# Attention and a long convolution in one kernel: zero columns by the planned share, kv cleared in pieces, kv stored in load order, part A in pairs

## The chip, the core and the metric

The kernel runs on one core of one Trainium2 chip. The metric is the device time of one execution in microseconds (us). The kernel before takes 856.5 us, the median of 7 runs (855.29 to 857.41).

## What is computed

Two independent parts write the two halves of the output's last axis. S is 2048, D is 640, and all data are bf16.

```
part A:  k_shift[t] = sum over j<4 of k[t-j] * shift_k[:, j]
         kv         = k_shift * v
         y          = causal convolution of kv with ssm_k, channel by channel, over 2048 steps (by FFT)
         a          = q * (y + kv * ssm_D)
part B:  q, k, v    = x @ wqkv, 32 heads of 20 channels
         p          = softmax(q k^T / sqrt(20)), 2048 x 2048 for each head
         b          = (p v) @ wo
output   = concat(a, b) on the last axis, (1, 2048, 1280)
```

## The kernel before, in words

**An order written by a planner.** The kernel is one straight program for each engine. While it is built, the class `Prog` keeps a modelled clock for each engine (`P.T`), and every operation is added with a modelled cost `c`. A loop (L1240) looks at the modelled clock of TensorE and decides what comes next on it. Once written, the order on every engine is fixed: if an operation is slower on the chip than its `c`, everything queued behind it on that engine is late. Nothing is rearranged at run time.

**Part B.** There are 512 blocks (4 query chunks of 512, 8 groups of 4 heads, 16 key blocks of 128), each with 4 units, one for each head: 2048 units in all. For a unit, TensorE computes scores of 128 keys by 512 queries into one PSUM bank (S_task, L619), and an exponential is taken of them. ScalarE does this for 2 or 3 banks in one instruction (EXP_task, L661). Some units are given to VectorE instead, which takes the exponential in six or seven steps: the first reads PSUM (L681), the others work in SBUF on two units at a time (`chain_end`, L711 to L721). The results lie in 36 slots of SBUF until PV_task (L739) multiplies them with v and frees the slots. `want_vec` (L1150) says when VectorE gets a unit: only if its modelled lead and backlog are below VQ us, and only in the earlier key blocks of a group (KBW, and KBV for a pair that is already open).

**Work beside it.** The projections for q, k and v (L473, L522), the short filter of part A ("C" tasks, L550, with a multiplication by v on VectorE, L570), the output projection (L825) and the long convolution (L974) have due times in blocks and are put between the scores. The C tasks are due at block KV0 + KVS * n for n = 0 to 19. C tasks multiply by diagonal matrices Dg, which GpSimd builds with one instruction (L592) from the identity and the filter's weights SK.

**The long convolution.** After the last projections of k and v, the space of the weights is used again (`conv_setup`, L915). 40 tasks of 128 matmuls each (5120 matmuls, L974) multiply Toeplitz pieces of ssm_k, loaded by DMA (`hk_load`, L938), with kv. kv goes through HBM: VectorE's products are stored as rows in `kvr_scratch` (L564), loaded back 80 channels at a time (`kvr_load`, L933) and regrouped on GpSimd (`kvx_build`, L943). In each matmul the moving operand has n = 16 - d positions for two halves; it is doubled by a second set of columns that are zeros (KVZ). The doubled columns add zeros to the neighbouring results: they change no value. Only the first matmul of a task has no such columns. Part of the tile for kv must be zero and is cleared by one GpSimd instruction (L926).

**Columns that keep TensorE streaming.** The planner counts how long TensorE streams columns in the last 3.4 us (`share`, L1221). Where there is slack and the count is below ZTH, it adds matmuls on a tile of zeros (`zeros`, L381); ahead of a convolution step it adds one if the count is below ZLO.

**Order on GpSimd and VectorE.** GpSimd operations of the convolution wait in a list and are put beside a VectorE operation that reads PSUM (`pool_beside`, L428). A VectorE step marked "two" (those in SBUF) is planned not to start while GpSimd is planned busy.

**Part A's end.** For each 160 channels, 16 tiles of q (128 rows by 160) are loaded, multiplied by y on GpSimd (L1015), and stored (`A_start`, L1003). Six tiles are allocated and four are in flight.

**SyncE** issues nearly all DMAs in the order written; each waits for its own semaphore's DMA before it. x is loaded transposed: four tiles of 128 rows, then three of 512 rows (L400 to L405).

Of the kernel before, what the change touches and what calls it, by code (L numbers as in the profile page):

```python
# [25 lines left out]
NAQ = 6  # L26
# [4 lines left out]
OBS = 20  # L31
NXB = 3
KBV, KBW, LONE = 13, 12, 16
CQ = 0.026
KV0, KVS, VQ, CONVE, ZTH, AGE, WAIT3 = 52, 2.5, 5, 80, 2.1, 40, 0.2
ZST = 6
# [4 lines left out]
PKX, PAT = 0.56, 0.42  # L41
DMAX = 2.0
ZSL, ZLO = 0.45, 1.8
# [43 lines left out]
class Prog:  # L87
# [140 lines left out]
    def dmas(self, eng, pairs, dsem, reads=(), writes=(), slow=1, turn=False):  # L228
# [18 lines left out]
        c = 0.475 * len(pairs)  # L247
# [29 lines left out]
def build_kernel(nc, A_q, A_k, A_v, A_shift_k, A_ssm_k, A_ssm_D, B_x, B_wqkv, B_wo, out):  # L277
# [3 lines left out]
    with ExitStack() as es:  # L281
# [30 lines left out]
        HK_E, KVR_E, KVX_E, Y_E, AST_E = 4 * HKW, 64 * 80, 16 * 64, 16 * 160, 160  # L312
# [37 lines left out]
        kvr_d = nc.dram_tensor("kvr_scratch", (S, D), BF16).ap()  # L350
# [49 lines left out]
        for t in range(4):  # L400
            x_load(t, 1)
        x_load(4, 4)
        w_load("sp", [(WKV, D, 2, 0, 160), (WKV, 0, 1, 80, 80), (WQ, 0, 0, 80, 80)], b_Wa, "wa")
# [81 lines left out]
        def prologue():  # L485

            def two(bw, bd):

                bd.w = [t for b in bw for t in b.w]
                bd.r = []  # L490
            for _ in range(ZST):
                zeros(0, 1, True)
            KQ_mm("K", 0, MISC, 0, 384)
            hq, hk = [Buf(), Buf()], [Buf(), Buf()]
            for i, (bk, eng) in enumerate(((4, "dve"), (3, "act"))):
                KQ_mm("Q", 0, bk, 256 * i, 256)
                if i == 0:
                    copy("act", KT[:, 0, 0:384], bank[MISC][:, 0:384], bkb[MISC], hk[0], 0.6)
                copy(eng, QT[:, 0, 256 * i:256 * (i + 1)], bank[bk][:, 0:256], bkb[bk], hq[i], 0.45)
            KQ_mm("K", 0, 5, 384, 128)  # L500
            copy("dve", KT[:, 0, 384:512], bank[5][:, 0:128], bkb[5], hk[1], 0.35)
            two(hq, b_QT[0])
            two(hk, b_KT[(0, 0)])
# [29 lines left out]
        d_kvr, d_sk, d_kext, d_small = DS("kvr"), DS("sk"), DS("kext"), DS("small")  # L533
# [6 lines left out]
        def C_task(c, h, bk):  # L540
# [18 lines left out]
            def after():  # L559
                if h < 4:  # L560
                    return
                for t in range(4):
                    bd = Buf()
                    P.dma("sp", ap(kvr_d, [[32 * D, 4], [-D, 32], [1, D]], (c * 512 + t * 128 + 31) * D), kvst[i][:, t, :],  # L564
                          d_kvst[i], reads=[b_kvst[i]], writes=[bd])
                    b_kvd.append(bd)
# [5 lines left out]
        def setup_pool():  # L572
# [3 lines left out]
            P.dma("sp", SK, ap(A_shift_k, [[KS, 128], [128 * KS, NCC], [1, KS]]), d_sk, writes=[b_SK])  # L576
            k_load(0)
            k_load(1)
# [13 lines left out]
            P.op("pool", lambda e: e.tensor_tensor(  # L592
                Dg, ap(ident, [list(ident.ap[0]), [0, KS], [0, NCC], [1, 128]]),
                ap(SK, [list(SK.ap[0]), [1, KS], [KS, NCC], [0, 128]]), ALU.mult), reads=[b_ident, b_SK], writes=[b_Dg], c=6.0)
# [320 lines left out]
        def conv_setup():  # L915
# [10 lines left out]
            P.op("pool", lambda e: e.memset(KVr[:, 0:48, :], 0.0), writes=[cv["KVr"]], c=48 * 80 * 0.00095)  # L926
# [6 lines left out]
        def kvr_load(b):  # L933
            P.dmas("sp", [(KVr[32 * a:32 * a + 32, 16 * a:64, :],
                           ap(kvr_d, [[D, 32], [32 * D, 64 - 16 * a], [1, 80]], 80 * b)) for a in range(4)],
                   d_kvr, reads=b_kvd, writes=[cv["KVr"]], slow=2)
# [6 lines left out]
        def kvx_build(t):  # L943
            i = t % 2
            for h in range(2):
                dst = sub(KVX[i].bitcast(U32), [[64, 4], [16, 4], [1, 16]], 256 * h)
                src = sub(KVr2, [[1, 4], [40, 4], [160, 16]], t % 5 * 8 + 4 * h)
                pool_work(lambda e, dst=dst, src=src: e.tensor_copy(dst, src), [cv["KVr"]], [cv["KVX"][i][h]], PKX,  # L948
                          lambda h=h: kvr_load(t // 5 + 1) if h and t % 5 == 4 and t < 39 else None)
# [5 lines left out]
        def conv_task(bt):  # L955
# [3 lines left out]
            for u in range(4):  # L959
# [3 lines left out]
                for x in range(4):  # L963
                    for k in range(8):
# [6 lines left out]
                        rhs = sub(KVX[i], [[(2 - i) * KVX_E - p, 1 if st else 2], [64, 2], [2, n]], p)  # L971
                        o = sub(bank[MISC], [[-16 if u + x else 16, 1 if st else 2], [256, 2], [1, n]], (4 * u + x) * 16 + d)
                        yield (CQ, rd if x + k == 0 else [])
                        P.op("pe", lambda e, o=o, lhsT=lhsT, rhs=rhs, st=st, k=k: e.matmul(  # L974
                            o, lhsT, rhs, start=st, stop=k == 7, skip_group_check=True),
                            reads=rd, writes=[bkb[MISC]], tok=last, c=CQ, st=4 * n / 2400)
# [22 lines left out]
        def A_load(B, tp):  # L999
            i = tp % NAQ  # L1000
            P.dma("sp", Aq[i], ap(q2, [[D, 128], [1, 160]], tp * 128 * D + 160 * B), d_aq[i], writes=[cv["Aq"][i]])

        def A_start(B):  # L1003

            def go(tp):
                i = tp % NAQ
                q = cv["Aq"][i]
                A_load(B, tp)

                def after():  # L1010
                    P.dma("sp", ap(out2, [[2 * D, 128], [1, 160]], tp * 128 * 2 * D + 160 * B), Aq[i], d_ao[i], reads=[q])
                    if tp + NAQ - 2 < 16:
                        go(tp + NAQ - 2)

                pool_work(lambda e, a=Aq[i], y=Y[B % 2][:, tp, :]: e.tensor_tensor(a, a, y, ALU.mult), [q, cv["Y"][B % 2]], [q], PAT,  # L1015
                          after)

            for tp in range(NAQ - 2):
                go(tp)
# [99 lines left out]
        def dve_run(until):  # L1119
            while True:  # L1120
# [8 lines left out]
                if True:  # L1129
                    fn, rd, wr, c, two = w.steps[w.i]  # L1130
                    t = last_dve[0]
# [289 lines left out]
```

## Time and profile before

| what | value |
|---|---|
| median of 7 runs | 856.5 us |
| the profiled execution | 855.89 us |
| its span on the core | 853.2 us (2.7 us lie around it) |
| first exponential starts | 10.19 us |
| last exponential ends | 843.8 us |
| mean granted TensorE clock | 0.994 |
| exponentials on ScalarE | 465 of 2 units, 276 of 3, 1 of 1 (1759 units) |
| exponentials on VectorE | 289 units |
| convolution on TensorE | from 238.1 to 802.2 us |
| matmuls on zeros (L381) | 230 |
| HBM traffic | 106.83 MB read, 10.61 MB written |

"Span" is from the first to the last instruction. A row of a group of instructions gives: line, engine, operation, the tiles written and read, the shape, the count, then busy time in us and mean ns of one, then the idle time of the engine just before them and what ended it. In rows of the timeline, the numbers are start in us, length in us; square brackets hold the engine's idle time before it. Names such as R stand for the big working space, PS for PSUM, XV and XF for VectorE's own tiles. A busy share of TensorE says little here, since each matmul's record lasts some 390 ns for 512 columns while the next one starts about 215 ns later.

### The profile page before, as it was taken

What the parts mean: (1) busy time and instruction counts of PE and PEld (TensorE: products, weight loads), DVE (VectorE), ACT (ScalarE), POOL (GpSimd) and SP (SyncE); (2) the same over time, 40 slices, a digit from 0 to 9 for tenths busy, and PEclk for the clock granted to TensorE, in tenths of its full rate; (3) what the DMA queues carried; (4) which work ended last, traced back from release to release, by engine and by line L of the source; (5) the groups of instructions that cost most, each with busy time, mean ns of one, the idle gap of its engine ahead of it and who ended that gap; (6) DMA issues with size and microseconds to landing.
All of it is one profiled execution on the core that took longest, in us unless ns stands there. A gap on an engine that the chain in (4) does not pass through costs nothing.

```text
span 853.2 us, 27281 instructions
## 1 busy us (share of the span) xinstructions
PE 819.1 (96%) x11683; PEld 380.6 (45%) x11694; DVE 775.2 (91%) x1560; ACT 811.1 (95%) x748; POOL 96.6 (11%) x160
## 2 busy tenths in 40 slices
PE   8979999999999999999999999999999999999997
PEld 3433433442255454444534544554544554455422
DVE  2388999999989999998999999999999999999992
ACT  5878799999999999999999999999999999999996
POOL 2020000000111000012211010220110121100011
PEclk9989999999999999999999999999999999999999
DMA  9920211211749977978888796789798888988411
GB/s 182 292 61 2 42 54 22 73 33 32 145 111 204 179 171 171 186 167 186 193 163 175 166 209 140 175 199 195 176 188 158 199 191 194 164 185 181 77 31 46
DMA packets 189463, 121.91 MB, mean 143 GB/s; under 512 B 98048, under 2 KB 188672, under 8 KB 189344
## 3 DMA queue, kind: packets, MB, share of 16 engines
q1 hardware_dynamic: 187152, 117.06, 64.5%
q0 software_dynamic: 736, 2.75, 0.9%
q8 instruction: 92, 1.51, 0.8%
q10 hardware_dynamic: 1456, 0.37, 0.2%
q14 instruction: 27, 0.22, 0.1%
HBM read 106.83 MB, written 10.61 MB: 138 GB/s over the span
## 4 chain that ended last, share of the span: by engine, by line
PE 50%; ACT 33%; DVE 15%; issue 1%; DMA 0%; SPq 0%; DVEq 0%
ACT R L661 33%; PE PS L974 17%; PE PS L619 15%; PE PS L739 7%; PE PS L473 5%; DVE XV L681 4%; DVE XF L721 2%; PE PS L825 2%; PE PS L381 1%; PE PS L522 1%; DVE XF L716 1%; DVE R L711 1%; DVE ZS L991 1%; DVE ZS L990 1%; DVE R L993 1%
## 5 line engine op out<-in xcount | busy, mean ns | idle before, releaser
L661 ACT ACTIVATE R<-PS 128x1024 bf16<-128x1024 f32 (+1 forms) x742 | 807.6, 1232 | 26.8 <-PE PS L619 25.2
L619 PE MATMUL PS<-QT,KT 20*128 20x512 bf16 x2048 | 288.3, 386 | 19.2 <-ACT R L661 6.9
L974 PE MATMUL PS<-R 128*128 128x60 bf16 (+4 forms) x5120 | 212.1, 195 | 0.2 <-DVE R L993 0.2
L681 DVE TENSOR_SCALAR XV<-PS 128x512 uint16<-128x512 f32 x289 | 197.2, 684 | 16.0 <-PE PS L619 13.3
L974 PEld LDWEIGHTS PS<-R 128*128 128x128 bf16 x5120 | 176.0, 98 | 79.0 <-issue 77.7
L739 PE MATMUL PS<-R,V_sb 128*21 128x512 bf16 x2048 | 168.2, 385 | 5.3 <-DVE R L711 2.5
L619 PEld LDWEIGHTS PS<-QT,KT 20*128 20x128 bf16 x2048 | 71.9, 91 | 192.8 <-ACT R L661 132.9
L721 DVE TENSOR_TENSOR XF<-XF 128x1024 bf16<-128x1024 bf16 x145 | 98.7, 682 | 0.3
L718 DVE TENSOR_TENSOR XF<-XF 128x1024 bf16<-128x1024 bf16 x145 | 98.2, 681 | 0.2
L948 POOL COPY R<-R 128x256 uint32<-128x256 uint32 x80 | 51.1, 639 | 377.5 <-DVE XF L721 114.1
L739 PEld LDWEIGHTS PS<-R,V_sb 128*21 128x21 bf16 x2048 | 37.8, 89 | 78.3 <-issue 40.6
L381 PE MATMUL PS<-Zt 128*128 128x512 bf16 x230 | 68.5, 393 | 1.6 <-DVE Zt L375 1.0
L716 DVE TENSOR_SCALAR XF<-XV 128x1024 uint16<-128x1024 uint16 x145 | 64.5, 452 | 0.2
L711 DVE TENSOR_TENSOR R<-XF,XV 128x1024 uint16<-128x1024 bf16 x92 | 62.8, 685 | 0.2
L719 DVE TENSOR_SCALAR XF<-XF 128x1024 bf16<-128x1024 uint16 x145 | 60.2, 417 | 0.4
L717 DVE TENSOR_SCALAR XF<-XF 128x1024 bf16<-128x1024 uint16 x145 | 59.7, 418 | 0.1
L473 PE MATMUL PS<-xT,WQ 128*20 128x512 bf16 (+1 forms) x660 | 50.0, 380 | 0.9 <-DVE XV L681 0.7
L473 PE MATMUL PS<-xT,R 128*20 128x512 bf16 (+2 forms) x660 | 47.8, 382 | 1.8 <-DMA xT<-in_B_x_dram 1.3
L1015 POOL TENSOR_TENSOR R<-R 128x160 bf16<-128x160 bf16 x64 | 31.2, 488 | 160.6 <-DVE XF L719 50.8
L713 DVE TENSOR_TENSOR R<-XF,XV 128x512 uint16<-128x512 bf16 x105 | 40.4, 418 | 0.1
L462 DVE CAST KT<-PS 128x512 bf16<-128x512 f32 (+1 forms) x32 | 21.6, 675 | 13.8 <-PE PS L473 13.4
L749 DVE CAST OT_sb<-PS 128x512 bf16<-128x512 f32 x32 | 21.8, 681 | 12.8 <-PE PS L739 12.8
(54 smaller groups left out, 359.8 us busy)
## 6 DMA issues: line engine op xcount, KB each, us to landing
R<-kext_scratch SPq DMA_DIRECT2D x640, 136.0 KB, 3.7
R<-in_A_v_dram SPq DMA_DIRECT2D x4, 640.0 KB, 6.2
kext_scratch<-in_A_ssm_k_dram POOLq DMA_DIRECT2D x1, 2560.0 KB, 13.3
kvr_scratch<-R SPq DMA_DIRECT2D x16, 160.0 KB
R<-kvr_scratch SPq DMA_DIRECT2D x8, 320.0 KB, 6.1
R<-in_A_q_dram SPq DMA_DIRECT2D x64, 40.0 KB, 3.4
out_dram<-R SPq DMA_DIRECT2D x64, 40.0 KB, 2.8
R<-kvr_scratch SPq DMA_DIRECT2D x8, 240.0 KB, 7.0
```

What stands on the lines that cost most here:

```text
L381: P.op("pe", lambda e: e.matmul(bank[bk], Zt, zrhs, start=start, stop=start, skip_group_check=True), reads=[b_Zt], writes=[bkb[bk]], tok=s ...
L473: ins = e.matmul(bank[bk][32 * i:32 * i + DH, 0:n], Wt[:, cc, off + i * DH:off + (i + 1) * DH], xT[:, cc, x0:x0 + n], start=(cc == 0), sto ...
L619: ins = e.matmul(bank[b0 + i], KT[32 * u:32 * u + DH, g, kb * 128:(kb + 1) * 128], QT[32 * u:32 * u + DH, qs(qc, g), :], start=True, stop= ...
L661: P.op("act", lambda e: e.activation(P_sb[:, s0:s0 + m, :], PS[:, b0 * 512:(b0 + m) * 512].rearrange("p (u q) -> p u q", u=m), ACT.Exp, sc ...
L681: work(0.2, [(lambda e: e.tensor_scalar(V, bank[bk], scale * 1.4426950408889634 * 128.0, 127.0 * 128.0, op0=ALU.mult, op1=ALU.add), [bkb[b ...
L711: last = [(lambda e: e.tensor_tensor(o, Q2, V2, ALU.add), bv + [bq], [b_P[z] for z in zs], two, True)]
L716: (lambda e: e.tensor_scalar(F.bitcast(U16), V, 127, None, op0=ALU.bitwise_and), bv, [bf], one, True),
L718: (lambda e: e.tensor_tensor(Q, Q, F.bitcast(U16), ALU.mult), [bf, bq], [bq], two, True),
L719: (lambda e: e.tensor_scalar(F, F.bitcast(U16), a / 16384.0, b / 128.0, op0=ALU.mult, op1=ALU.add), [bf], [bf], one, True),
L721: (lambda e: e.tensor_tensor(Q, Q, F, ALU.mult), [bf, bq], [bq], two, True)] + last, end)
L739: ins = e.matmul(bank[OBANK][32 * u:32 * u + DH + 1, :], V_sb[:, kb, 4 * g + u, :], P_sb[:, slot[4 * b + u], :], start=first, stop=last, t ...
L974: P.op("pe", lambda e, o=o, lhsT=lhsT, rhs=rhs, st=st, k=k: e.matmul(o, lhsT, rhs, start=st, stop=k == 7, skip_group_check=True), reads=rd ...
```

## The change

The computation is the same. These parts change.

1. **Convolution matmuls** are doubled with zero columns only for d = 1 and 2, and only if `share` is below ZDU = 2.1 at that point. They are costed at CQ = 0.0258 (not doubled) or CQD = 0.0304 (doubled), where all had 0.026.
2. **Planner constants.** The filling of zeros: ZTH 2.1 to 2.2, ZLO 1.8 to 1.4, ZSL 0.45 to 0.3. C tasks: KV0 52 to 56, KVS 2.5 to 3.0. Convolution paced to end 100 units before the end, not 80. VectorE units: VQ 5 to 5.5, KBV 13 to 12. GpSimd costs: PKX 0.56 to 0.64, PAT 0.42 to 0.49. The accumulation bank may be used for early tasks until unit 28, not 20 (OBS). Transposing DMAs are costed by rows.
3. **Opening.** x is loaded by 256, 256, 512, 512, 512 rows. SK is loaded right after the third of these; before, it came after all weights. q and k of the first group are projected in two halves of 256, each behind its own half of x, with 7 and 4 zero matmuls ahead; ScalarE copies k and VectorE copies q.
4. **GpSimd's opening.** Dg is built ahead of GpSimd's DMAs, directly after its first memsets; the second load of k and v moves behind the small loads on SyncE.
5. **kv in HBM** is laid out as 8 channel groups x 32 x 64 x 80. A store of one row tile becomes 8 DMAs of 160-byte pieces (128 DMAs in all, where there were 16 with rows of 1280 bytes). A load reads one contiguous run for each partition (2.5 to 10 KB), where it read runs of 160 bytes.
6. **The kv tile is cleared** in four GpSimd instructions that `pool_beside` places, not in one.
7. **Part A in pairs:** two tiles of q share one load and one store (32 of each, where there were 64); three pairs are allocated, two in flight.

```diff
-KBV, KBW, LONE = 13, 12, 16
-CQ = 0.026
-KV0, KVS, VQ, CONVE, ZTH, AGE, WAIT3 = 52, 2.5, 5, 80, 2.1, 40, 0.2
-ZST = 6
+KBV, KBW, LONE = 12, 12, 16
+CQ, CQD, ZDU = 0.0258, 0.0304, 2.1
+KV0, KVS, VQ, CONVE, ZTH, AGE, WAIT3 = 56, 3.0, 5.5, 100, 2.2, 40, 0.2
+ZST = 7, 4
...
-PKX, PAT = 0.56, 0.42
+PKX, PAT = 0.64, 0.49
...
-ZSL, ZLO = 0.45, 1.8
+ZSL, ZLO = 0.3, 1.4
...
-        c = 0.475 * len(pairs)
+        c = 0.475 * len(pairs) if not turn else 0.4 + 0.0068 * pairs[0][1].shape[0]
...
-        kvr_d = nc.dram_tensor("kvr_scratch", (S, D), BF16).ap()
+        kvr_d = nc.dram_tensor("kvr_scratch", (8, 32, 64, 80), BF16).ap()
...
-        for t in range(4):
-            x_load(t, 1)
+        x_load(0, 2)
+        x_load(2, 2)
         x_load(4, 4)
+        d_sk = DS("sk")
+        P.dma("sp", SK, ap(A_shift_k, [[KS, 128], [128 * KS, NCC], [1, KS]]), d_sk, writes=[b_SK])
...
-            for _ in range(ZST):
-                zeros(0, 1, True)
-            KQ_mm("K", 0, MISC, 0, 384)
             hq, hk = [Buf(), Buf()], [Buf(), Buf()]
-            for i, (bk, eng) in enumerate(((4, "dve"), (3, "act"))):
-                KQ_mm("Q", 0, bk, 256 * i, 256)
-                if i == 0:
-                    copy("act", KT[:, 0, 0:384], bank[MISC][:, 0:384], bkb[MISC], hk[0], 0.6)
-                copy(eng, QT[:, 0, 256 * i:256 * (i + 1)], bank[bk][:, 0:256], bkb[bk], hq[i], 0.45)
-            KQ_mm("K", 0, 5, 384, 128)
-            copy("dve", KT[:, 0, 384:512], bank[5][:, 0:128], bkb[5], hk[1], 0.35)
+            for i, (bq, bk) in enumerate(((4, MISC), (3, 5))):
+                for _ in range(ZST[i]):
+                    zeros(i, 1, True)
+                KQ_mm("Q", 0, bq, 256 * i, 256)
+                copy("dve", QT[:, 0, 256 * i:256 * (i + 1)], bank[bq][:, 0:256], bkb[bq], hq[i], 0.45)
+                KQ_mm("K", 0, bk, 256 * i, 256)
+                copy("act", KT[:, 0, 256 * i:256 * (i + 1)], bank[bk][:, 0:256], bkb[bk], hk[i], 0.45)
...
-                    P.dma("sp", ap(kvr_d, [[32 * D, 4], [-D, 32], [1, D]], (c * 512 + t * 128 + 31) * D), kvst[i][:, t, :],
-                          d_kvst[i], reads=[b_kvst[i]], writes=[bd])
+                    P.dmas("sp", [(ap(kvr_d, [[80, 4], [-5120, 32], [1, 80]], ((32 * n + 31) * 64 + 16 * c + 4 * t) * 80),
+                                   kvst[i][:, t, 80 * n:80 * n + 80]) for n in range(8)], d_kvst[i], reads=[b_kvst[i]], writes=[bd])
...
-            P.op("pool", lambda e: e.memset(KVr[:, 0:48, :], 0.0), writes=[cv["KVr"]], c=48 * 80 * 0.00095)
+            for i in range(4):
+                pool_work(lambda e, i=i: e.memset(KVr2[:, 480 * i:480 * i + 480], 0), [], [cv["KVr"]], 0.55)
...
-                        rhs = sub(KVX[i], [[(2 - i) * KVX_E - p, 1 if st else 2], [64, 2], [2, n]], p)
-                        o = sub(bank[MISC], [[-16 if u + x else 16, 1 if st else 2], [256, 2], [1, n]], (4 * u + x) * 16 + d)
+                        m = 2 if d in (1, 2) and share(P.T["pe"]) < ZDU else 1
+                        rhs = sub(KVX[i], [[(2 - i) * KVX_E - p, m], [64, 2], [2, n]], p)
+                        o = sub(bank[MISC], [[-16 if u + x else 16, m], [256, 2], [1, n]], (4 * u + x) * 16 + d)
...
-                            reads=rd, writes=[bkb[MISC]], tok=last, c=CQ, st=4 * n / 2400)
+                            reads=rd, writes=[bkb[MISC]], tok=last, c=CQ if m == 1 else CQD, st=2 * m * n / 2400)
```

## The prediction

> **What bounds the kernel now.** I read the slices of the page first, then the groups, then stretches, and last the timeline where ScalarE is idle.
>
> ```profile
> DVE  2388999999989999998999999999999999999992
> ACT  5878799999999999999999999999999999999996
> ...
> PEclk9989999999999999999999999999999999999999
> ```
>
> ScalarE is short of full in the first five slices (to 107 us) and in the last. VectorE is nearly full after them. TensorE's clock dips once, in the third slice.
>
> ```profile
> L661 ACT ACTIVATE R<-PS 128x1024 bf16<-128x1024 f32 (+1 forms) x742 | 807.6, 1232 | 26.8 <-PE PS L619 25.2
> L974 PE MATMUL PS<-R 128*128 128x60 bf16 (+4 forms) x5120 | 212.1, 195 | 0.2 <-DVE R L993 0.2
> L381 PE MATMUL PS<-Zt 128*128 128x512 bf16 x230 | 68.5, 393 | 1.6 <-DVE Zt L375 1.0
> L948 POOL COPY R<-R 128x256 uint32<-128x256 uint32 x80 | 51.1, 639 | 377.5 <-DVE XF L721 114.1
> ```
>
> The exponentials on ScalarE wait for nothing but scores (L619). In the trace, back to back, they start every 0.905 us (two units) and 1.331 us (three): 465 and 276 of them make 788.2 us. From 10.2 us to 843.8 us is 833.6 us, so about 45 us are lost: 20 before 106 us and 25 after (these lie above the idle time, since a late start also loses the overlap of some 0.11 us). ScalarE is the bound; what counts is what makes scores late, and how many units VectorE takes.
>
> The stretches (columns: TensorE, weight loads, VectorE, ScalarE, GpSimd, clock, DMA share, GB/s):
>
> ```profile
> 50.00:64.00 14.00, 9.36 (x88) 3.17 (x86) 12.75 (x20) 8.32 (x9) 5.55 (x3) 0.76 0.03 3
> 79.00:92.00 13.00, 12.98 (x201) 6.37 (x193) 12.09 (x23) 5.62 (x6) 0.00 (x0) 1.00 0.01 3
> 520.00:832.00 312.00, 301.26 (x4568) 149.23 (x4568) 302.24 (x617) 308.91 (x274) 44.79 (x80) 1.00 0.79 166
> ```
>
> Two short stretches hold 13 us of idle ScalarE; the long one, 312 us, holds 3. The timeline of the two:
>
> ```profile
> 52.51 5.41 DVE L716 TENSOR_SCALAR XF<-XV 128x1024 uint16<-128x1024 uint16 x1
> 52.99 4.63 POOL L592 TENSOR_TENSOR R<-ident,SK 128x2560 bf16<-128x2560 bf16 x1
> 58.29 0.61 PE L619 MATMUL PS<-QT,KT 20*128 20x512 bf16 x3 [4.16 <-DVE V_sb L527]
> 58.95 1.02 ACT L661 ACTIVATE R<-PS 128x1024 bf16<-128x1024 f32 x1 [3.75 <-PE PS L619]
> 61.42 1.02 ACT L661 ACTIVATE R<-PS 128x1024 bf16<-128x1024 f32 x1 [1.45 <-PE PS L619]
> ...
> 83.76 3.28 ACT L661 ACTIVATE R<-PS 128x1536 bf16<-128x1536 f32 x3 [3.01 <-PE PS L619]
> 90.43 0.61 PE L739 MATMUL PS<-R,V_sb 128*21 128x512 bf16 x8
> 91.42 1.94 ACT L661 ACTIVATE R<-PS 128x1024 bf16<-128x1024 f32 x2 [4.37 <-PE PS L619]
> ```
>
> First: GpSimd builds Dg, and a VectorE step that takes 0.45 us elsewhere takes 5.41 us. TensorE waits 4.16 us, loses its clock, and ScalarE waits 3.75 + 1.45 + 0.48 us. Second: TensorE runs only projections and C tasks for some 5 us twice; scores resume after a PV (L739) that waited for VectorE.
>
> **The change, part by part.** The sum is made against 855.9 us, the profiled execution; the median is 0.6 us above it.
>
> *Dg moved to the opening.* It leaves the two-input GpSimd instruction out of VectorE's way: 3.75 + 1.45 + 0.48 = 5.7 us of idle ScalarE. Nothing else is done in that gap, so everything after it moves up. In its new place it waits for SK, now issued at some 7 us; its record at the old place took from 19.1 to 26.5 us behind large loads. With 4.63 us of work it ends between 15 and 20 us. Behind it on GpSimd is only the fill of the filter's scratch, which itself waited 15.25 us for x until 19.75; the scratch is first read at 213 us. VectorE then has only copies from PSUM (chains start after unit 60, near 28 us). The nearest row is L681, PSUM reads of 0.68 us each that ran beside the clearing at 213 us undisturbed. Cost 0 taken; if these copies were blocked, up to 4.2 us come back. Gain 5.4 (1.5 to 6.5).
>
> *Opening.* The four x loads of one tile were issued from 0.74 to 6.04 us (1.3 each), and the fourth landed at 7.70. A load of four tiles issues in 2.71 to 3.43, so a pair takes some 1.9 and the second pair lands near 6.5. What follows (two projections of 0.55, a copy, scores) is as long as now, 2.5 us to the first exponential at 10.19. But four zero matmuls stand before the second half; cold they cost 0.43 each. Gain 1.0 (0 to 1.6). A second piece: the first long projection at 11.59 us ran at half clock (2.31 us where others take 1.26), and ScalarE waited 1.44. More zeros ahead may hold the clock: 0.7 (0 to 1.4).
>
> *C tasks four blocks later and three apart.* They do the same work (16 matmuls, 1.0 us each, and L570, 0.68). The gaps at 83.76 and 91.42 are where they meet the projections. The space after them was full: between 107 and 213 us ScalarE idled 1.1 of 106. Gain 3.5 of 7.4 (0 to 7). What is late next: the last C task comes about 12 blocks later, at 1.6 us a block some 20 us, and its stores behind it, so the convolution may start 10 to 15 us later than 238.1 and stops 8 us earlier. That makes it 4% denser; no wait follows while TensorE has slack.
>
> *Stores of kv in pieces of 160 bytes.* 128 instructions where there were 16, at 0.5 us each on SyncE: 56 us more issue. The four stores of a chunk already wait for one another (40.3 us over 12 waits). Queued behind them are only the loads of later k and v and then the convolution's first loads; nobody else until 213 us. Here the Trainium skill speaks against the change: "DMA: Bandwidth & Descriptors", its opening table, says that transfers below 512 B do not reach line rate. By the rule every store is slow; by the rows, loads of kv in the same 160-byte runs (320 KB) landed in 6.1 us, and a 20 KB store is a sixteenth of that. Per group of four row tiles I take 4 x 6 = 24 us for 15, which is 9 us more before the convolution, within the shift above. Cost on the path 0 (0 to 1). The loads get shorter, but no matmul of L974 waited for a DMA (0.2 us of idle before 5120): gain 0.
>
> *Clearing in four.* The row of 3.30 us lay beside VectorE steps of usual length, and the gap after them was ended by a projection. Gain 0 (0 to 0.7). Pairs in part A: 64 DMAs less on a queue that nobody waits for: 0.
>
> *Convolution.* Pieces of 34 matmuls take 1.16 us in the chain: (1.16 - 0.195)/33 = 29.2 ns each, and 31.6 ns on average over the trace with short pieces, against 26 planned. So the scores behind a piece are 0.1 to 0.2 us later than planned. Without the second columns 32 to 26 columns stream. Here a rule weighs against the row: "TensorE: Matmul & The Clock Gate", section on the 56 ns gap, gives columns / 2.4 GHz plus 2.5 ns, but never under about 25 ns. By the rule the doubled forms (64, 60, 56, 52 columns) take 26.9 on average, single ones 25: 1.9 ns saved. By the row of 29.2 with the rule's floor it is 4; nothing is saved if the weight load sets the pace. I take 26 to 27 for single ones: with some 1500 of 5120 still doubled, 3600 x 3 to 5 ns = 11 to 18 us of TensorE, off the path. What reaches ScalarE: of 25 us lost after 106 us, by my walk back through the trace 7.4 lie behind a convolution piece, 7.3 behind a PV, 2.6 behind zeros. With planned costs near the measured ones (0.639 and 0.488 on GpSimd also) half of the first and a quarter of the second go: 5.5. Against it, 3600 matmuls less some 29 columns each are 43 us of streaming, and ZTH goes up, so up to 200 more zero matmuls (0.22 each) come in, and their lateness grows from 2.6 by 2. Gain 3.5 (-4 to 9).
>
> *VQ and KBV.* They pull in opposite ways on VectorE's 289 units; VectorE is full (302 of 312). A unit more spares 0.45 us of ScalarE. Net 0 (-2 to 3).
>
> Sum: 5.4 + 1.0 + 0.7 + 3.5 + 3.5 = 14.1. 855.9 - 14.1 = 841.8; with the median's 0.6, 842.4.
>
> **Rivals.**
>
> *A, the sum holds:* 842, chance 0.58, range 836 to 849. *B, only the opening gains* (Dg, first loads, clock) and the full engines give nothing, since each us won by scores returns as a wait for VectorE's chains: 856.5 - 7.1 = 849.4, chance 0.22. For it: VectorE at 97%. Against it: the 7.4 us of two clear gaps. *C, all upper halves:* 6 + 1.5 + 1 + 6 + 8 = 22.5, 834, chance 0.07. *D, gains are given back* by lateness of another order: 856, chance 0.04.
>
> *E, slower: the clock.* In the convolution TensorE streams fewer columns, and the filling is only a plan. The granted clock of 0.96 over 10.2 to 50 us and 0.76 over 50 to 64 us means some 3.3 and 6.7 us at half clock, the second after a wait of 4.16 us; after it ScalarE waited 1.9 us more. A window of 3.4 us at half clock puts TensorE (from 240 to 800 us its start-to-start times fill 96%, some 90% without the zeros) about 1.5 us behind. Nine or ten such windows take back 14 us; from there on it is slower. With 16 (10% of the convolution's 165) it would be 856.5 - 14 + 24 = 866. For it: zero columns are a fifth of what streams there. Against it: the doubled case returns as soon as the planned share is under 2.1 of 3.4 us, and zeros are added below 2.2. Chance 0.09.
>
> **How the numbers follow.** The likeliest is A, 842. A, B and C make faster by over 0.2% (what a measurement here can tell): 0.87; D 0.04; E 0.09. The range 831 to 854 takes in A, B, C and leaves out D and E.
>
> **What would show it.** Dg within the first 22 us and no VectorE step over 1.5 us; clock 1.0 in the third slice; the first exponential near 9 us; ScalarE's idle time before L661 from 26.8 to some 13 us; more than 300 matmuls on zeros; convolution pieces nearer 27 ns. It is wrong if the clock falls below 1 in the convolution, if VectorE's units fall well below 280, or if the gaps of 79 to 92 us reappear later.

## The result, and the profile after

Over 12 executions the changed kernel took 848.3 to 910.8 us, median 873.4; the kernel before took 856.6 (median of 30, 855.3 to 860.3), so the usual outcome is 17 us slower. In ten of the twelve the mean granted clock was 0.885 to 0.960 (864.9 us and more), and in two it was 0.984 (849.3 and 848.3). Executions at a low clock are elsewhere set aside as disturbed, and the two alone give a ratio of 0.9907 (95%: 0.9887 to 0.9928), or 848.6 us; here the low clock is an effect of the change, as the experiments show. So both numbers are kept in view: 848.6 at best, 873.4 as a rule. (Line numbers moved: scores are L617 now, PV L737, exponentials L659 on ScalarE and L679 on VectorE, the convolution L975, v times the C result L569.)

The profiled execution took 874.52 us, with a span of 872.3. First the page of the changed kernel: its slices, then the groups.

```profile
DVE  1399999999956696899999999999999999999993
ACT  5899998999876797899999999999999999999996
...
PEclk9999999999955596799999999999999999999999
...
L659 ACT ACTIVATE R<-PS 128x1024 bf16<-128x1024 f32 (+1 forms) x748 | 806.4, 1259 | 46.4 <-PE PS L617 42.0
...
L975 PE MATMUL PS<-R 128*128 128x32 bf16 (+5 forms) x5120 | 198.7, 186 | 2.2 <-issue 2.0
...
L381 PE MATMUL PS<-Zt 128*128 128x512 bf16 x239 | 73.3, 405 | 2.1 <-DVE Zt L375 1.0
```

The clock, which dipped once before, now falls to half in the 12th to 14th slice and once more in the 16th and 17th. ScalarE's idle time before the exponentials rose from 26.8 to 46.4 us. The matmuls on zeros are 239, hardly more than the 230 of before. 2101 of the 5120 convolution matmuls were still doubled, so the tests of `share` left only part of them thin.

The stretches of the changed kernel (columns as in the prediction):

```profile
50.00:64.00 14.00, 13.98 (x164) 5.07 (x163) 13.82 (x33) 14.00 (x15) 0.00 (x0) 1.00 0.06 22
...
79.00:92.00 13.00, 12.71 (x163) 4.95 (x163) 12.96 (x27) 12.10 (x12) 0.00 (x0) 1.00 0.01 1
...
238.00:307.00 69.00, 65.11 (x537) 21.66 (x539) 41.93 (x85) 47.33 (x43) 5.95 (x11) 0.51 0.45 100
307.00:334.00 27.00, 24.37 (x444) 12.94 (x440) 23.53 (x50) 24.92 (x22) 2.58 (x4) 1.00 0.94 196
334.00:358.00 24.00, 24.00 (x260) 8.17 (x256) 15.55 (x31) 17.20 (x16) 1.90 (x3) 0.51 0.62 130
...
520.00:832.00 312.00, 303.34 (x4852) 148.98 (x4854) 307.26 (x635) 311.86 (x287) 44.82 (x79) 1.00 0.86 181
```

The two stretches that held the lost time before are repaired: from 50 to 64 us ScalarE is busy 14.00 of 14, and from 79 to 92 us 12.10 of 13. From 238 to 307 us TensorE's clock is 0.51 and it passes half as many matmuls as before (537, where the same stretch of before has 1073); ScalarE is busy 47.33 of 69. From 334 to 358 us it happens again. The long stretch after 520 us is slightly better than before (311.86 of 312).

What stands at the start of the half-clock stretch is seen in the timeline of the changed kernel around 240 us:

```profile
235.71 1.60 SPq L234 DMA_DIRECT2D kvr_scratch<-R  x3
...
240.00 1.94 ACT L659 ACTIVATE R<-PS 128x1024 bf16<-128x1024 f32 x2 [3.79 <-DMA kvr_scratch<-R]
...
241.08 0.60 PE L617 MATMUL PS<-QT,KT 20*128 20x512 bf16 x2 [3.88 <-ACT R L659]
```

Three of the stores of kv in pieces are the last to be issued (1.60 us). At 240.00 an exponential starts after a wait of 3.79 us for the landing of those stores, and at 241.08 TensorE's next score starts after 3.88 us without a matmul. It waits for the exponential, because PSUM is full. The clock record shows half clock from 238.7 on.

Why an exponential waits for a store is seen in the program. When `conv_setup` has run, the old space of weights and C products is given to new users, and the first of the 36 slots for exponentials lie on it. The loop puts these slots on the free list at once (`if not added and conv_k is not None`), with `cv["dead"]`, every use of the old space, as what they must wait for. The stores read their data from that space. The planner does model when a store lands, but from the start of the first DMA of a group and by its bytes only: 1.7 + 160/215 + 0.5 + 2.0 = 4.9 us for a tile, the same for one DMA as for eight (`dmas` and `op` in the class `Prog`). So the slots looked free in time. The waits of SyncE, then of ScalarE, in the changed kernel (total, times, longest):

```profile
SPq L234 <- DMA kvr_scratch<-R: 30.4, 12, 2.8
```

```profile
ACT R L659 <- PE PS L617: 42.0, 63, 3.7
...
ACT R L659 <- DMA kvr_scratch<-R: 3.8, 1, 3.8
```

The 8 stores of one row tile take about 4.35 us to issue and some 2.6 more to land before the next 8 may start, 6.9 us a tile where 4.9 are planned. Before, one store of a tile took 3.7, within the plan. Four tiles of a chunk follow one another, so the last is some 8 us later than planned.

### The profile page after: what moved, and what is told of

It reads as the page before. It is cut to its first block, busy times and chain, and to the rows that moved or that the text cites. A ratio compares the mean times of both kernels' runs of the same rounds, so it can differ in the third digit from the quotient of the medians.

```text
span 872.3 us, 27413 instructions
## 1 busy us (share of the span) xinstructions
PE 840.8 (96%) x11693; PEld 371.8 (43%) x11703; DVE 775.4 (89%) x1599; ACT 809.7 (93%) x754; POOL 95.0 (11%) x163
## 4 chain that ended last, share of the span: by engine, by line
PE 36%; ACT 32%; DVE 23%; SPq 3%; DMA 3%; issue 2%; DVEq 0%; ACTq 0%
ACT R L659 32%; PE PS L617 11%; PE PS L975 7%; PE PS L737 6%; DVE XV L679 5%; PE PS L475 5%; SPq L234 3%; DMA kvr_scratch<-R 3%; DVE XF L716 3%; DVE XF L719 3%; PE PS L823 2%; PE PS L381 2%; PE PS L521 2%; DVE R L709 2%; DVE XF L717 2%
## 5 line engine op out<-in xcount | busy, mean ns | idle before, releaser
L659 ACT ACTIVATE R<-PS 128x1024 bf16<-128x1024 f32 (+1 forms) x748 | 806.4, 1259 | 46.4 <-PE PS L617 42.0
L617 PE MATMUL PS<-QT,KT 20*128 20x512 bf16 x2048 | 302.1, 400 | 16.9 <-ACT R L659 8.8
L679 DVE TENSOR_SCALAR XV<-PS 128x512 uint16<-128x512 f32 x292 | 197.8, 683 | 29.8 <-PE PS L617 28.2
L975 PEld LDWEIGHTS PS<-R 128*128 128x128 bf16 x5120 | 164.3, 98 | 90.5 <-issue 89.9
L975 PE MATMUL PS<-R 128*128 128x32 bf16 (+5 forms) x5120 | 198.7, 186 | 2.2 <-issue 2.0
L737 PE MATMUL PS<-R,V_sb 128*21 128x512 bf16 x2048 | 172.0, 399 | 2.3 <-DVE R L711 1.0
L617 PEld LDWEIGHTS PS<-QT,KT 20*128 20x128 bf16 x2048 | 72.9, 91 | 203.9 <-ACT R L659 148.0
L719 DVE TENSOR_TENSOR XF<-XF 128x1024 bf16<-128x1024 bf16 (+1 forms) x150 | 100.2, 669 | 0.5
L716 DVE TENSOR_TENSOR XF<-XF 128x1024 bf16<-128x1024 bf16 (+1 forms) x150 | 100.1, 669 | 0.2
L737 PEld LDWEIGHTS PS<-R,V_sb 128*21 128x21 bf16 x2048 | 36.8, 90 | 75.2 <-issue 43.6
L717 DVE TENSOR_SCALAR XF<-XF 128x1024 bf16<-128x1024 uint16 (+1 forms) x150 | 61.6, 412 | 0.2
L715 DVE TENSOR_SCALAR XF<-XF 128x1024 bf16<-128x1024 uint16 (+1 forms) x150 | 61.5, 412 | 0.1
L714 DVE TENSOR_SCALAR XF<-XV 128x1024 uint16<-128x1024 uint16 (+1 forms) x150 | 60.7, 410 | 0.3
L711 DVE TENSOR_TENSOR R<-XF,XV 128x512 uint16<-128x512 bf16 x124 | 48.2, 418 | 0.2
L475 PE MATMUL PS<-xT,R 128*20 128x512 bf16 (+1 forms) x660 | 46.3, 375 | 1.0 <-DVE R L569 1.0
L464 DVE CAST QT<-PS 128x512 bf16<-128x512 f32 (+1 forms) x33 | 22.0, 667 | 14.0 <-PE PS L475 13.8
L464 DVE CAST KT<-PS 128x512 bf16<-128x512 f32 x31 | 21.2, 684 | 11.6 <-PE PS L475 11.5
## 6 DMA issues: line engine op xcount, KB each, us to landing
kext_scratch<-in_A_ssm_k_dram POOLq DMA_DIRECT2D x1, 2560.0 KB, 13.8
```

Of the source, the lines that this page charges most:

```text
L475: ins = e.matmul(bank[bk][32 * i:32 * i + DH, 0:n], Wt[:, cc, off + i * DH:off + (i + 1) * DH], xT[:, cc, x0:x0 + n], start=(cc == 0), sto ...
L617: ins = e.matmul(bank[b0 + i], KT[32 * u:32 * u + DH, g, kb * 128:(kb + 1) * 128], QT[32 * u:32 * u + DH, qs(qc, g), :], start=True, stop= ...
L659: P.op("act", lambda e: e.activation(P_sb[:, s0:s0 + m, :], PS[:, b0 * 512:(b0 + m) * 512].rearrange("p (u q) -> p u q", u=m), ACT.Exp, sc ...
L679: work(0.2, [(lambda e: e.tensor_scalar(V, bank[bk], scale * 1.4426950408889634 * 128.0, 127.0 * 128.0, op0=ALU.mult, op1=ALU.add), [bkb[b ...
L715: (lambda e: e.tensor_scalar(Q, F.bitcast(U16), -128.0, None, op0=ALU.add), [bf], [bq], one, True),
L716: (lambda e: e.tensor_tensor(Q, Q, F.bitcast(U16), ALU.mult), [bf, bq], [bq], two, True),
```

## The experiments

**Theory 1** says: the stores in pieces are late, the exponentials into the slots above them wait, TensorE runs dry for 3.9 us and loses its clock, and a TensorE that is only fully occupied at half speed doesn't get it back for long. **Theory 2**, the forecast's rival E, says: the thin convolution lets too few columns stream, and the clock falls by itself. Where two kernels are compared, medians of the executions are meant.

**Stores in rows again, all else kept.** The loads follow the layout and read runs of 160 bytes again (the edit of `kvr_load` is left out below).

```diff
-        kvr_d = nc.dram_tensor("kvr_scratch", (8, 32, 64, 80), BF16).ap()
+        kvr_d = nc.dram_tensor("kvr_scratch", (S, D), BF16).ap()
...
-                    P.dmas("sp", [(ap(kvr_d, [[80, 4], [-5120, 32], [1, 80]], ...
+                    P.dma("sp", ap(kvr_d, [[32 * D, 4], [-D, 32], [1, D]], ...
```

> The changed kernel, with kv stored in whole rows and loaded in 160-byte runs, as before; all else is as changed. Theory 1 (the stores of kv in small pieces land late, the exponential that takes over their space waits 3.8 us, TensorE idles and its clock falls to half for tens of us): no wait of an exponential for the stores, granted clock about 0.99, all executions within 1% of one another, near 838 to 845 us. Theory 2 (the matmuls with fewer columns leave TensorE too thinly used, so that any hiccup drops the clock): the clock still falls in the convolution, the times still spread over 2% or more, to 860 us and above.

Measured: 832.8 to 834.7 us in four executions, 850.1 in the fifth; median 834.6, ratio 0.9734 (0.9721 to 0.9748). One part of the change cost 14 us at its best and about 39 by the medians. The profiled execution was the fifth, and its stretches show the second theory's event:

```profile
600.00:650.00 50.00, 48.68 (x821) 25.69 (x819) 48.97 (x105) 49.88 (x46) 5.11 (x8) 1.00 0.83 181
650.60:694.90 44.30, 44.30 (x408) 16.64 (x408) 29.76 (x59) 31.65 (x29) 2.50 (x4) 0.50 0.59 123
```

From 650.6 us on the clock is at half for 44 us, though in the 50 us before it nothing was idle: VectorE and ScalarE were full, and no gap of TensorE was longer than 0.55 us. So theory 1 takes most of the loss, and a drop without a stall exists.

**Everything doubled, all else kept.** Every convolution matmul but the first of a task has its zero columns again, costed at the new 0.0304.

```diff
-                        m = 2 if d in (1, 2) and share(P.T["pe"]) < ZDU else 1
+                        m = 1 if st else 2
```

> The changed kernel with every convolution matmul doubled with zero columns again (but the first of a task), costed at 0.0304 us; kv in pieces as changed. Theory 1: the wait of some 4 us near 240 us stays and starts a half-clock stretch as it does in the changed kernel, since it lies ahead of the convolution; times spread as there, 848 to 900 us. Theory 2: the times draw together at 845 to 852 us and the clock is 0.98 or more in nearly all executions.

Measured: 845.4 to 859.9 us, median of 11 857.1, ratio 0.9955 (0.9916 to 0.9994). An exponential still waits 3.77 us for the stores at 239.09, and half clock follows from 240.7 to 288.5 us. More columns shorten what follows and narrow the spread; they don't take the trigger away.

**The slots later.** Only the moment at which the slots are put on the free list is moved, until the first of the 40 convolution tasks has begun; the stores stay in pieces.

```diff
-            if not added and conv_k is not None:
+            if not added and conv_k is not None and conv_b >= 1:
```

> The changed kernel with kv in pieces, but the four slots of the exponentials that lie on the old space are given free only once the first convolution task has been started, some tens of us later. Theory 1: the wait for the stores is gone, the clock holds, 838 to 846 us in nearly all executions, as with kv in rows. Theory 2: the spread stays, with some executions above 860 us.

Measured: 835.5 to 836.5 us in all four executions, median 835.9, ratio 0.9757 (0.9743 to 0.9770). The page of this kernel, then its stretches:

```profile
ACT  5899999799999999999999999999999999999996
...
PEclk9999999999999999999999999999999999999999
...
L659 ACT ACTIVATE R<-PS 128x1024 bf16<-128x1024 f32 (+1 forms) x747 | 800.5, 1264 | 14.4 <-PE PS L617 13.7
```

```profile
107.00:213.00 106.00, 103.87 (x1200) 41.12 (x1196) 102.80 (x205) 100.03 (x98) 0.00 (x0) 1.00 0.26 46
213.00:250.00 37.00, 35.55 (x407) 10.97 (x404) 36.69 (x76) 36.71 (x37) 2.29 (x5) 1.00 0.43 80
250.00:520.00 270.00, 264.39 (x4314) 130.96 (x4310) 264.74 (x545) 268.73 (x251) 35.27 (x59) 1.00 0.89 190
```

The clock never leaves full speed after 15 us, and ScalarE's idle time before the exponentials is 14.4 us, where 26.8 were before and 46.4 after. The stretch from 213 us, where the changed kernel stalled, is full. There are as many thin matmuls as in the changed kernel (3046 not doubled here, 3019 there): thin columns alone didn't drop the clock here. Theory 1 holds.

**The kernel before with the stores in pieces** (and the loads in long runs that go with them), nothing else.

> The kernel before with one part of the change alone: kv stored in 160-byte pieces and loaded in long runs. The prediction's step: nothing on the path, 856 to 858 us. Theory 1: the stores land late here too, an exponential waits for them some 4 us near 210 to 230 us, and a half-clock stretch follows; with doubled columns it is 860 to 872 us, with times that spread.

Measured: 869.2 to 871.6 us in five executions, 884.9 in one, median 871.0, ratio 1.0151 (1.0123 to 1.0179). The timeline of this kernel near 178 us:

```profile
178.47 0.69 DVE L570 TENSOR_TENSOR R<-PS,R 128x512 bf16<-128x512 f32 x1 [3.69 <-DMA kvr_scratch<-R]
...
180.56 1.45 ACT L661 ACTIVATE R<-PS 128x1536 bf16<-128x1536 f32 x1 [3.60 <-PE PS L619]
```

Here VectorE's product of v and C (L570) waits for the store, for one of the buffers that the store is still reading; the exponential behind it waits for scores, 3.60 us. At 230.84 the first door opens as in the changed kernel: an exponential waits 3.68 us for the store itself, and TensorE 3.77 us for the exponential. Half clock goes with each (179.2 to 192.9 and 230.4 to 237.3). So the stores in pieces hurt by two doors, and both stand in the kernel before.

**C tasks at the times of before**, with the stores in pieces and the slots later.

```diff
-KV0, KVS, VQ, CONVE, ZTH, AGE, WAIT3 = 56, 3.0, 5.5, 100, 2.2, 40, 0.2
+KV0, KVS, VQ, CONVE, ZTH, AGE, WAIT3 = 52, 2.5, 5.5, 100, 2.2, 40, 0.2
```

> The version with the slots given free later (835.9 us), with the C tasks due as before (KV0 52, KVS 2.5). The prediction gave the later times 3.5 us: then 839 to 840 us. In the traces the waits of 79 to 92 us went with Dg alone, so I now expect 834 to 837 us, no difference.

Measured: 846.7 to 862.5 us, median of 12 857.1, ratio 0.9945 (0.9908 to 0.9981), 21 us above the kernel with the slots later, where no difference was expected. The timeline of this kernel near 184 us:

```profile
182.87 3.25 SPq L234 DMA_DIRECT2D kvr_scratch<-R  x6
184.47 1.49 DVE L569 TENSOR_TENSOR R<-PS,R 128x512 bf16<-128x512 f32 x2 [4.93 <-DMA kvr_scratch<-R]
...
185.22 0.61 PE L475 MATMUL PS<-xT,R 128*20 128x512 bf16 x4 [4.49 <-DVE R L569]
...
186.41 1.02 ACT L659 ACTIVATE R<-PS 128x1024 bf16<-128x1024 f32 x1 [4.17 <-PE PS L617]
```

The other door opens: six stores are being issued, VectorE waits 4.93 us for a buffer, TensorE 4.49 us for VectorE, ScalarE 4.17 us for TensorE, and half clock follows from 184.2 to 201.3. With stores of 6.9 us a tile (28 us for four), the C times of before leave too little room between the products; the later ones leave enough. This door isn't all of the 21 us. In the profiled executions the kernel loses 11 us more of ScalarE than the one with the slots later between 100 and 200 us, and as much again elsewhere: half clock lasts from 13.6 to 23.8 us in place of 3.4 us, and it comes back from 249.1 to 255.9, after TensorE had waited 2.28 us for GpSimd's regrouping of kv at 249.40.

**Dg alone**, in the kernel before: SK loaded early, Dg built in the opening.

> The kernel before with one part of the change alone: SK is loaded after the third load of x and Dg is built on GpSimd ahead of its DMAs. The prediction's step: the VectorE step of 5.41 us and the three gaps of ScalarE after it go, 5.4 us less (1.5 to 6.5): 851 us. If instead the planner's new order brings its own gaps, the gain is under 2 us: 855 us. The clock should be 0.996 (one cold window of 3.4 us in place of three).

Measured: median 851.5 (850.7 to 853.0), ratio 0.9939 (0.9925 to 0.9952). The stretch from 50 to 64 us is full (ScalarE 14.00 of 14), and so is the one from 79 us (12.41 of 13). The timeline of ScalarE in this kernel, from 139 to 155 us, shows what is late next:

```profile
141.52 6.88 ACT L662 ACTIVATE R<-PS 128x1024 bf16<-128x1024 f32 x6 [1.83 <-PE PS L620]
152.42 2.85 ACT L662 ACTIVATE R<-PS 128x1024 bf16<-128x1024 f32 x3 [4.01 <-PE PS L620]
```

The planner's order shifted, and the same meeting of C tasks and projections now stands here, in a space that before was full.

**The planned cost of a convolution matmul alone**, in the kernel before: 0.0304 where 0.026 stood. And the same with Dg in the opening.

```diff
-CQ = 0.026
+CQ = 0.0304
```

> The kernel before with one number changed: a convolution matmul is costed at 0.0304 us where 0.026 was planned; all stay doubled. If planning with the measured cost is what takes away ScalarE's small waits from 250 us on (21.6 us lost there before, 9.6 in the version with the slots later): 846 to 850 us. If the columns themselves count, the planner only makes room by spreading: 854 to 858 us.

> The kernel before with two parts of the change: Dg built in the opening, and the planned cost of a convolution matmul at 0.0304 us (all stay doubled, everything else as before). If the gain of the whole change is these two: 857.1 - 5.7 - 13 = 838 us where the clock holds. If they overlap: 843 to 848 us. Whether the clock holds in all executions is open: with the cost alone it did not in most.

Measured: the cost alone 843.0 to 870.5 us, median of 12 851.7, ratio 0.9908 (0.9876 to 0.9940), with granted clocks from 0.952 to 0.997. With Dg early as well 838.2 to 839.2 in all five, ratio 0.9776 (0.9745 to 0.9807). On top of Dg the cost is worth 13.2 us. The page of the kernel with both:

```profile
ACT  5899999789999999999999999999999999999995
...
L662 ACT ACTIVATE R<-PS 128x1024 bf16<-128x1024 f32 (+1 forms) x743 | 799.9, 1289 | 17.6 <-PE PS L620 17.2
...
L381 PE MATMUL PS<-Zt 128*128 128x512 bf16 x163 | 48.4, 395 | 1.1 <-DVE Zt L375 1.0
```

ScalarE's idle time is down to 17.6 us with all columns doubled. The higher cost leaves the plan less slack, and it puts in only 163 matmuls on zeros (229 with Dg alone); what these alone are worth was not tried.

**Both repairs, and what the columns are worth.** The slots later and everything doubled; then rows and slots later; then all three.

> The version with the slots given free later (835.9 us), with every convolution matmul doubled again and costed at 0.0304. It is what the removed columns are worth when nothing stalls. If the shorter matmuls themselves count (28.3 ns on average against 31.6 measured, 5120 x 3.3 = 17 us of TensorE): 842 to 848 us. If it was only that the planned cost now fits the measured one, nothing is lost: 835 to 838 us. Clock 0.997 either way.

> The changed kernel with both repairs: kv in rows as before, and the four slots given free only with the first convolution task. Theory 1: neither repair adds to the other, 834 to 836 us, clock 0.997 or more in all executions. If the single half-clock stretch seen with kv in rows alone (650 to 690 us, one execution of five) comes from the thin columns, it comes back here in some executions, at about 850.

> Rows and later slots with every convolution matmul doubled. If the thin columns cause the remaining half-clock stretches: all executions within 835 to 840 us, clock 0.997 or more. If not: some executions at 843 to 850 us as without the doubling.

Measured: slots later and doubled 838.6 (836.6 to 839.2, ratio 0.9776, 0.9749 to 0.9803), 2.7 us above the thin version; the executions don't overlap, though the intervals do. Rows and slots later 842.0 (833.3 to 849.2; two of six at 833 to 834 with a clock of 0.997, four at 0.968 to 0.983; ratio 0.9783, 0.9738 to 0.9828). With doubling as well 840.5 (839.7 to 844.0, clock 0.990 or more, ratio 0.9807, 0.9774 to 0.9841). Rows make the best executions, and their clock isn't safe.

**More filling**: rows, slots later, ZTH 2.5, ZLO 2.0, ZDU 2.4.

> Rows and later slots (833.3 to 849.2 us, clock 0.968 to 0.998), with more filling: ZTH 2.5 for 2.2, ZLO 2.0 for 1.4, ZDU 2.4 for 2.1. If the remaining half-clock stretches come from too few streamed columns per window of 3.4 us: all executions within 833 to 839 us and clock 0.996 or more. If not: the spread to 849 stays.

Measured: 886.8 to 890.4 us, ratio 1.0365 (1.0333 to 1.0396), clock 0.994 or more. The stretches of this kernel:

```profile
520.00:820.00 300.00, 297.29 (x4379) 139.67 (x4383) 286.92 (x585) 299.78 (x275) 39.10 (x69) 1.00 0.74 161
820.00:874.00 54.00, 52.50 (x789) 32.41 (x787) 9.63 (x22) 0.34 (x1) 7.84 (x15) 1.00 0.85 172
```

The clock held, but 508 matmuls on zeros took the convolution's places. The exponentials are over at 820 us, as in the good kernels, and then TensorE works 54 us on a convolution that is left over while ScalarE has 0.34 us to do. Filling isn't free when it competes with work that only has to be done at some time.

## Why the prediction was right or wrong

Its sign and range hold for the undisturbed comparison (848.6, in 831 to 854). For the kernel as it usually runs they don't: the median of 873.4 is the outcome of rival E, with E's place (the convolution) and another trigger. That the best executions fall into the range is in part luck: the stores took 12.7 us that were put at nothing, and the planned cost brought 9.7 more than was put down for it.

**The stores: the step that failed.** The prediction put "Cost on the path 0 (0 to 1)", because queued behind the stores were only loads and "nobody else until 213 us". The time of a group was nearly right (24 us for four tiles forecast, some 28 measured), but by another way: the prediction took 6 us a tile from the landing of loads, and the trace has 4.35 us of issue and 2.6 of landing, where a store in rows took 0.5 and 3.2. So the rule of the Trainium skill that it set against the change ("DMA: Bandwidth & Descriptors", transfers below 512 B) pointed the right way, but it is the eight issues that cost the time here, and no row shows that the pieces themselves landed late. What the prediction missed are the waiters on other engines, those who want the memory that a store still reads, and that the plan would not know of the delay. There are two, the exponentials in the slots above (3.79 us at 240) and VectorE's products (0.96 us of TensorE at 190.11 in the changed kernel, 4 to 5 us with the earlier C times). Moving one `free.update` behind the first convolution task brings back 12.7 us of the best executions (848.6 to 835.9) and 37.5 of the medians.

Most of this isn't the wait but the clock behind it. From 200 to 360 us, which holds both stretches at half clock, ScalarE lost 41.8 us against its back-to-back pace, with the slots later 4.8. Of the 37.0 in between 3.8 are the wait; 33.2 over 92.2 us at half clock are 0.36 us for each. By this estimate the two good executions, whose mean clock of 0.984 means 27 us at half (0.016 x 847 / 0.5) for 3 with the slots later, lose 3.8 + 24 x 0.36 = 12.4, near the 12.7 measured; neither of the two was profiled. The kernel of before with pieces has 20.6 us at half behind its two waits of 3.6: 14.6 by the same price, 13.8 measured. Rival E had priced a window of 3.4 us at 1.5; the runs give 1.2. It asked for nine or ten windows to lose the gain; the trace shows 27, in two unbroken runs.

**Dg: right, and the sum in part by luck.** Forecast 5.4, measured 5.7 alone (857.1 to 851.5). The gap of 5.7 us is gone, as forecast. But with Dg alone the waits of 79 to 92 us went too, and ScalarE lost 8.4 us more than before between 100 and 200 us (10.4 for 2.0); the match comes out of all three. In the timeline of the changed kernel:

```profile
10.55 4.48 POOL L575 TENSOR_TENSOR R<-ident,SK 128x2560 bf16<-128x2560 bf16 x1 [6.05 <-DMA SK<-in_A_shift_k_dram]
```

It starts at 10.55 and ends at 15.0 us, the early end of the 15 to 20 forecast. The one copy from PSUM that VectorE made meanwhile (at 13.82) took 0.69 us, as long as later ones; with Dg alone, where Dg ran from 13.02 to 17.50, the copies beside it took the usual 0.69 and 0.33 us. (The 0.45 us that the prediction gives for VectorE's step elsewhere is a mean with the step of 5.41 us in it; without it, it is 0.42.)

**The opening: 1.7 forecast, nothing seen.** The first exponential started at 11.01 us in the changed kernel and at 10.04 with the slots later (before 10.19); from the first exponential to 50 us ScalarE lost 6.0 us with the slots later, as before. The half-clock stretch at 11 to 15 us is still there, and so is a wait of 1.44 us at 14.33 with the slots later. There the second pair of x landed at 6.94 us, not at 6.5, and the four zero matmuls held TensorE from 6.88 to 7.84 ahead of the second half's projections. The prediction names these matmuls, but its 1.0 us leaves too little for them: of 0.76 us won by the landing, 0.15 arrived. No kernel undid the opening alone.

**C tasks: between.** The gaps at 83.76 and 91.42 went, but they go with Dg alone as well, and return at 141.52 and 152.42. The later C times leave one of them, which the prediction had named as a sign of being wrong. In the timeline of ScalarE in the changed kernel:

```profile
150.82 1.94 ACT L659 ACTIVATE R<-PS 128x1024 bf16<-128x1024 f32 x2 [3.69 <-PE PS L617]
```

From 100 to 200 us ScalarE lost 2.0 us before, 10.4 with Dg alone and 7.3 with the later C times and the slots later: a gain of some 3.1 for 3.5 forecast, read from traces of kernels that differ in more than the C times. What the step didn't see is what the later times are needed for: with stores in pieces the kernel with the earlier ones is 21 us slower.

**The convolution's planned cost: the mechanism right, the size wrong.** The prediction took the difference between the planned 26 ns and the 31.6 of the trace as "half of the first and a quarter of the second", 5.5 us, less 2 for lateness of zeros: 3.5. The planned cost alone is worth 13.2. From 250 to 800 us ScalarE lost 21.4 us before, 10.6 with the cost put right and 9.7 with Dg as well. The plan didn't know of 5120 x 5.6 ns = 29 us of TensorE. The prediction looked for their effect in the waits behind convolution pieces and PVs alone; that they made late starts behind everything else too, or that the 66 to 80 fewer matmuls on zeros helped, is argued and not shown.

**Its columns: small.** Singles start 25 to 26 ns apart (median), doubled ones 30; the mean over the convolution fell from 31.6 to 28.3, or 17 us of TensorE, and this brought 2.7 us of time. The forecast of more than 300 matmuls on zeros was wrong (239), since doubling came back for 2101 matmuls, where 1500 were taken.

**VectorE's units, the clearing, the pairs:** 292 units for 289; the four clearings took 0.5 us each where one took 3.3; ScalarE waited for neither, nor for the pairs. At 0 as forecast, seen in the trace only.

The sum, with the stores' waiters away: 857.1 - 835.9 = 21.2 us, of which Dg 5.7, the planned cost 13.2, and 2.3 for all the rest together (the opening's 0.15, the C tasks' 3.1 and the columns' 2.7 come from other comparisons and need not add up to it). Two edits in the kernel before (838.3) hold nearly all of it.

**What stays open.** Thin columns alone: with them and no stall the clock held in four of four (slots later), fell in one of five (rows) and seems to have fallen in four of six (both); doubled, it held in fourteen of fifteen (three kernels, 0.994 or more) and was 0.990 in one execution. That speaks for a part of theory 2. But the kernel of before with the right cost is doubled as well and its clocks went from 0.952 to 0.997; its profiled execution, a good one (843.7), has half clock only from 58.2 to 68.5 us, after the old wait for Dg. What started the drops in its other executions no trace caught. The changed kernel's second drop follows a gap for which the profile names no engine:

```profile
329.81 1.01 PE L975 MATMUL PS<-R 128*128 128x60 bf16 x30
332.80 0.23 PE L975 MATMUL PS<-R 128*128 128x32 bf16 x2 [1.99 <-issue]
```

TensorE stands still for 1.99 us before 332.80, put down to "issue", and from 334.3 to 358.2 the clock is at half. The record of the DMAs has a hint. On the page of the changed kernel:

```profile
q8 instruction: 93, 1.52, 0.8%
```

These are 93 transfers of 16 KB, on average one for every 256 instructions of TensorE (matmuls and weight loads). The one that started at 329.92 came 434 instructions after the one before, by this count later than any other of this kernel, and TensorE went on 2.88 us after it had started. The runs have two other gaps put down to "issue" above 0.7 us, one with the slots later (until 303.51) and one with the C times of before (until 297.59). Both ended 2.77 us after the start of such a transfer that was among the latest of its kernel. So TensorE seems to have stood without instructions; why the transfer was late stays open, and no run tried it.

## What to carry to other kernels

When a store gets slower, list who wants to write the memory that it reads, on every engine, beside who is queued behind it. A stall on TensorE is priced by the clock that it loses and not by its own length: here 3.8 us of waiting cost 12.7 us at best and 37 by the medians. And in a kernel whose order is planned, hold each planned cost against the trace before anything else: 6.9 us for 4.9 on 16 groups of stores and 31.6 ns for 26 on 5120 matmuls decided more here than any edit to the work itself.

## What the runs showed of the hardware

The granted clock has a memory. Counted in windows of 3.41 us as the clock record has them, with 512 columns taken as 215 ns at full clock and twice that at half, full clock was kept in all windows but one that streamed for 0.47 of the time or more (the one is that of 0.52 ahead of the drop with the stores in rows), and the windows ahead of a drop in the changed kernel had 0.29 to 0.43. At half clock, windows of 0.70 to 0.88 in the changed kernel (the one with the gap in it aside) stayed at half, and in all runs it was left after 0.81 to 0.93. So in these runs about half a window of columns was enough at full clock, and at half clock a TensorE whose records fill 65 of 69 us stayed there for 68 us. The Trainium skill, "TensorE: Matmul & The Clock Gate", in its table of the two states, has full clock return after one busy window of about 3.4 us; by that rule, if windows as full as these count as busy, the drop at 238.7 would have cost one or two windows. The trace has twenty, and it decides.

A gap of 2.0 us was followed by the loss of the clock as well (at 330.8), so a stall need not fill a window; in the kernel before, TensorE worked on projections during 5 us without scores and kept its clock. And in the kernel before, the matmul behind a doubled one of 52 or 64 columns started 32.8 ns after it (mean at full clock), behind one of 56 or 60 columns 30.3: the shorter was not the faster.
